# Attention inside an attention + MoE + MLP kernel: the reciprocal sums are transposed and multiplied onto the value products, instead of multiplying the exponentials

## The chip, the cores and the metric

One core of one Trainium2 chip runs the whole program. The metric is the device time of one execution, in microseconds (us). Times come from three timed runs of the kernel before and from one further execution that the hardware profiler recorded. Engines: TensorE (PE, with its weight loads as PEld), VectorE (DVE), ScalarE (ACT), GpSimd (POOL), and SyncE (SP), which issues most DMAs.

## The reference

```
B, H, S, D = 2, 8, 576, 64                      # attention
scores = q @ k.T / sqrt(D) + (cum[q] - cum[k])  # cum = cumsum(log(clip(f)))
scores = where(causal, -1e9, scores)
attn = exp(scores - max(scores))
attn = attn / (sum(attn) + 1e-9)
x = attn @ v                                    # -> [1152 tokens, 512]
p = domain_probs / sum(domain_probs)            # MoE: 4 experts, 512 -> 1024 -> 512
x = sum_e p[:, e] * (relu(x @ w1[e]) @ w2[e])
h = x @ w_in; g = h * sigmoid(1.702 * h)        # MLP: 512 -> 2048 -> 512
return g @ w_out
```

The step that the change touches is the division by the row sum: the kernel before divides the exponentials, the changed one divides `attn @ v`.

## The kernel before, in words

The tokens form four chunks `c`: 256 and 320 tokens of each of the two batches. Attention goes by pairs of heads, in three passes: chunk 0 (four pairs), chunk 1 (four pairs), then chunks 2 and 3 together (four pairs). A pair is cut into units. In chunk 0 a unit is one head with two tiles of 128 queries. In the other chunks a unit is one tile of 128 queries for both heads of the pair; the last tile of chunks 1 and 3 holds 64 queries of each head and is 576 keys wide (here "the 576 unit"; the units before it are the 384 and the 512 unit, after the width of their scores).

The generator `attention()` advances by one unit per step ("pull"). Step `i` emits, in this order: the value product `emit_pv` and the hand-over `emit_x2` of a pair whose last unit was `i-3`; the transposes `emit_tr` of unit `i-2`; exponential `emit_exp` and normalisation `emit_norm` of unit `i-1`; scores `emit_scores` and the maximum pass `emit_max` of unit `i`. So the exponentials of a unit are transposed two steps after its scores. Also in that step the keys, queries and decay rows of a pair three units ahead are prepared on GpSimd (`prep_parts`: tiles `khi`, `klo`; `prep_queries`: `qhi`, `qlo`; `prep_cum`: tiles `cb`, `cbs`, whose rows come by a broadcast DMA from `cumd` and get the causal triangle added), and the next pair's inputs are loaded on SP's queue.

For one unit the chain is: scores (PE, tile `s`), maximum with the decay added (DVE, `e`, `mx`), exponential with its sum (ACT, `e`, `sm`), sum + 1e-9 and its reciprocal (DVE, L454 and L455), multiplication of the exponentials by it (POOL, L457), transposes (PE, tile `t`, L475), copies to `ph` (ACT, in chunk 0 half of them DVE), and per pair the value product (PE, tile `x`, L505), rounding to `xh` (ACT), remainder `xl` (DVE, L514).

Between pulls the main loop emits expert products. Each is twelve matmuls in three groups of four (high parts, low weights, low activations). The weights come as `wst` by DMA and are split: the high part `whi` on ACT or POOL, the low part `wlo` on DVE (L165). `emit_first` is a block of 48 products that stands after the eleventh pull. After attention only expert and MLP products are left.

TensorE executes in the order of the program text. The other engines' orders are set by a scheduler at compile time; each engine then runs its list strictly in order, so an instruction that waits holds up all behind it.

Of the kernel before, what the change touches and what calls it, by code (L numbers as in the profile page):

```python
# [7 lines left out]
F32 = mybir.dt.float32  # L8
# [3 lines left out]
ALU = mybir.AluOpType  # L12
# [3 lines left out]
NT = B * S  # L16
DM = 512
SA = 256
SB = S - SA
CH = [(0, 0, SA), (0, SA, SB), (1, 0, SA), (1, SA, SB)]  # L20
NCH = len(CH)

WN = 384
WIDE = [NCH, NCH + 1, NCH + 2]
KW = S + 128
# [8 lines left out]
def attn_moe_mlp(ctx: ExitStack, tc: tile.TileContext, qk0, qk1, qk2, v0, vp, fg, dp, wa_moe, wb_moe, wa_mlp, wb_mlp, outT):  # L34
# [6 lines left out]
    nc = tc.nc  # L41

    def pool(name, bufs, space=None, scope=ctx):
        kw = {} if space is None else {"space": space}
        return scope.enter_context(tc.tile_pool(name=name, bufs=bufs, **kw))

    def f(ap):
        return ap.bitcast(F32)
# [4 lines left out]
    def round_act(out, in_):  # L53
        nc.scalar.activation(out=out, in_=in_, func=AF.Copy)  # L54

    const = pool("const", 1)
# [5 lines left out]
    tmp_p = pool("tmp", 2)  # L62
# [6 lines left out]
    xh, xl = ([t[:, :, t0:t0 + n] for t0, n in span] for t in (xh_t, xl_t))  # L69
# [11 lines left out]
    att_scope = ctx.enter_context(ExitStack())  # L81
    ac = pool("ac", 1, scope=att_scope)
    hi_p = pool("hi", 2, scope=att_scope)
    qhi_p = pool("qhi", 3, scope=att_scope)
    kq_p = pool("kq", 3, scope=att_scope)
    v_p = pool("v", 3, scope=att_scope)
    cb_p = pool("cb", 4, scope=att_scope)
    cbs_p = pool("cbs", 2, scope=att_scope)
    e_p = pool("e", 3, scope=att_scope)
# [159 lines left out]
        dpb[e] = t  # L249

    def load_probabilities():
        raw = const.tile([128, NT // 32], F32, name="dpraw")
        nc.sync.dma_start(out=raw, in_=dp)
        return raw

    def make_probabilities(raw):

        out = const.tile([128, 4, NT // 128], F32, name="dpn")
        s = const.tile([128, NT // 128], F32, name="dps")
        v = raw.rearrange("p (j e) -> p e j", e=4)  # L260
        nc.gpsimd.tensor_add(s, v[:, 0], v[:, 1])
        for e in (2, 3):
            nc.gpsimd.tensor_add(s, s, v[:, e])
        nc.gpsimd.tensor_scalar(out=s, in0=s, scalar1=1e-9, scalar2=1.0, op0=ALU.add, op1=ALU.mult)
        nc.vector.reciprocal(out=s, in_=s)
        nc.gpsimd.tensor_mul(out, v, s.unsqueeze(1).to_broadcast([128, 4, NT // 128]))
        nc.sync.dma_start(out=dpT.rearrange("e (p j) -> p e j", p=128), in_=out)
# [23 lines left out]
    def plain(c):  # L291


        return c == 0
# [24 lines left out]
    def load_heads(p, h0):  # L319

        cs, b, s0 = p
        st = pairs[p, h0] = {}
        src = (qk2 if b else qk1)[h0 // 2]
        st["kq"] = kq_p.tile([128, KW], F32, tag="kq", name="kq")
        nc.sync.dma_start(out=st["kq"], in_=src[:, :KW])
        for i, c in enumerate(cs):
            st["q", c] = kq_p.tile([128, QW], F32, tag="qr", name="qr")
            nc.sync.dma_start(out=st["q", c], in_=src[:, KW + i * QW:KW + i * QW + QW])
        st["vd"] = v_p.tile([128, 5, 2, D], F32, tag="vd", name="vd")
        nc.sync.dma_start(out=st["vd"], in_=vp[b * H // 2 + h0 // 2].rearrange("p (t g d) -> p t g d", t=5, g=2))  # L330

# [17 lines left out]
    def prep_cum(p, h0):  # L349

        cs, b, s0 = p
        st = pairs[p, h0]
        r = b * H + h0
        st["cb"] = []
        for g in range(2):
            cb = cb_p.tile([128, 896], F32, tag="cb", name="cb")
            nc.sync.dma_start(out=cb[:, :512], in_=cumd[r + g:r + g + 1, :512].to_broadcast([128, 512]))

            nb = (384 - s0) // 128
            nc.gpsimd.tensor_add(cb[:, 512 + s0:896].rearrange("p (t k) -> p t k", t=nb),  # L360
                                 cb[:, s0:384].rearrange("p (t k) -> p t k", t=nb),
                                 tri.unsqueeze(1).to_broadcast([128, nb, 128]))
            nc.gpsimd.tensor_add(cb[:, 384:512], cb[:, 384:512], tri)
            st["cb"].append(cb)
        st["cbs"] = cbs_p.tile([128, S], F32, tag="cbs", name="cbs")
        nc.sync.dma_start(out=st["cbs"], in_=cumd[r:r + 2, :].unsqueeze(1).to_broadcast([2, 64, S]))
        for g in range(2):
            z = slice(64 * g, 64 * g + 64)
            nc.gpsimd.tensor_add(st["cbs"][z, 512:], st["cbs"][z, 512:], tri[z, z])
# [81 lines left out]
    def emit_norm(c, u):  # L451
        e, sm, todo = sc[c, u]
        k = len(todo)
        nc.vector.tensor_scalar(out=sm[:, 1, :k], in0=sm[:, 0, :k], scalar1=1e-9, scalar2=None, op0=ALU.add)  # L454
        nc.vector.reciprocal(out=sm[:, 0, :k], in_=sm[:, 1, :k])  # L455
        for i, (q0, off, w, _) in enumerate(todo):
            nc.gpsimd.tensor_scalar(out=e[:, off:off + w], in0=e[:, off:off + w], scalar1=sm[:, 0, i:i + 1],  # L457
                                    scalar2=1.0, op0=ALU.mult, op1=ALU.mult)

    def emit_tr(c, u):  # L460

        hs, tiles = u
        s0 = CH[c][1]
        e, sm, todo = sc.pop((c, u))
        for h in hs:
            if (c, h) not in ph_of:
                ph_of[c, h] = pt_p.tile([128, 4, SB], F32, tag="ph", name="ph")
        for k, (q0, off, w, _) in enumerate(todo):
            o = q0 - s0
            nk = (w + 127) // 128  # L470

            for k0, k1 in [(0, min(nk, 4))] + [(4, 5)] * (nk > 4):
                pt = ps_t.tile([128, 512], F32, tag="t", name="t")
                for i in range(k0, k1):
                    nc.tensor.transpose(pt[:, 128 * (i - k0):128 * (i - k0) + 128], e[:, off + 128 * i:off + 128 * i + 128], ident)  # L475
                cols = pt[:, :128 * (k1 - k0)].rearrange("p (i q) -> p i q", q=128)
                for j, h in enumerate(hs if w == S else hs[k:k + 1] if len(hs) > 1 else hs):
                    r = 64 if w == S else 128
                    ph = ph_of[c, h]
                    ph = ph[:, 3:4, 0:64] if k0 else ph[:, 0:k1, o:o + r]  # L480
                    if plain(c) and k1 == 2:
                        nc.vector.tensor_copy(ph, cols[:, :, j * r:(j + 1) * r])
                    else:
                        round_act(ph, cols[:, :, j * r:(j + 1) * r])
# [22 lines left out]
    def emit_x2(c, h):  # L507
        n = CH[c][2]
        if h % 2 == 1:
            k = h // 2  # L510
            x = xf.pop((c, k))[:, :n]
            x_made[0] += 1
            round_act(xh[c][:, k, :], x)
            nc.vector.tensor_sub(xl[c][:, k, :], x, f(xh[c][:, k, :]))  # L514

    STAGES = dict(scores=0, max=0, exp=1, norm=1, tr=2, pv=3, x2=3)
    L_X2 = STAGES["x2"]
# [5 lines left out]
    def attention():  # L523


        seq = unit_seq
        first, last = {}, {}
        for i, (c, u) in enumerate(seq):
            for h in u[0]:
                first.setdefault((pass_of[c], h - h % 2), i)  # L530
                last[c, h] = i
        first = {k: i for k, i in first.items() if k[0][2] or k[0][1]}
        first_q = {}
        for i, (c, u) in enumerate(seq):
            if not plain(c):
                first_q.setdefault((pass_of[c], u[0][0], c), i)
        nxt = list(first)
        per_unit = dict(scores=emit_scores, max=emit_max, exp=emit_exp, norm=emit_norm, tr=emit_tr)
        by_last = dict(pv=emit_pv, x2=emit_x2)
        names = sorted(STAGES, key=lambda k: -STAGES[k])  # L540
        for i in range(len(seq) + L_X2 + 1):
            done = None
            new = [k for k in nxt if first[k] == i + LEAD]
            for k in new:
                prep_parts(*k)
            for k in [k for k, j in first_q.items() if j == i + LEAD]:
                prep_queries(*k)
            for k in new:
                prep_cum(*k)
            for k in names:  # L550
                j = i - STAGES[k]
                if k in per_unit:
                    if 0 <= j < len(seq):
                        per_unit[k](*seq[j])
                    continue
                fn, at = by_last[k], last
                for key in list(at):
                    if at[key] == j:
                        fn(*key)
                        if k == "x2" and key[1] == H - 1:  # L560
                            done = key[0]
            for k in new:
                n = nxt.index(k) + 1
                if n < len(nxt):
                    load_heads(*nxt[n])
            yield done
# [162 lines left out]
    for i, (kind, v_, b, c) in enumerate(seq):  # L729
# [6 lines left out]
        for g in range(4):  # L736
            ev = early[g] if i == 0 else (emit_l1 if kind == 1 else emit_l2)(v_, b, c, g)
            n = 0
# [82 lines left out]
```

## Time and profile before

| | |
|---|---|
| time, median of 3 runs | 764.94 us (764.49 to 766.62) |
| the profiled execution: time, span from first to last instruction | 763.8 us, 762.1 us |
| busy in the span: PE, PEld, DVE, ACT, POOL | 714.2, 684.2, 457.7, 270.5, 293.4 us |
| mean granted TensorE clock, share of full | 0.989 |

The span is what the trace covers; the profiled execution's own time is 1.7 us longer than it, and 1.1 us shorter than the median. Busy time of PE counts overlapping matmuls once. Every instruction of an engine has a start, a duration, and, where the engine sat idle before it, the instruction whose end released it.

### The profile page before, as it was taken

What the parts mean: (1) busy time and instruction counts of PE and PEld (TensorE: products, weight loads), DVE (VectorE), ACT (ScalarE), POOL (GpSimd) and SP (SyncE); (2) the same over time, 40 slices, a digit from 0 to 9 for tenths busy, and PEclk for the clock granted to TensorE, in tenths of its full rate; (3) what the DMA queues carried; (4) which work ended last, traced back from release to release, by engine and by line L of the source; (5) the groups of instructions that cost most, each with busy time, mean ns of one, the idle gap of its engine ahead of it and who ended that gap; (6) DMA issues with size and microseconds to landing.
All of it is one profiled execution on the core that took longest, in us unless ns stands there. A gap on an engine that the chain in (4) does not pass through costs nothing.

```text
span 762.1 us, 11987 instructions
## 1 busy us (share of the span) xinstructions
PE 714.2 (94%) x4488; PEld 684.2 (90%) x4488; DVE 457.7 (60%) x1023; ACT 270.5 (35%) x629; POOL 293.4 (38%) x377
## 2 busy tenths in 40 slices
PE   4597778988999999999989999999999999999998
PEld 2375667977899999999989999999999999999998
DVE  4475366655674899999989934433893234324422
ACT  4355443455653223332122122212354443323420
POOL 6785666487342202232224423233352322222220
PEclk9998899999999999999999999999999999999999
DMA  9774354422133555545434311000100000000012
GB/s 300 216 194 149 125 145 140 128 99 67 56 111 89 187 164 180 183 139 164 116 108 139 110 56 56 1 0 1 56 1 1 1 1 1 0 1 1 1 42 83
DMA packets 31225, 68.81 MB, mean 90 GB/s; under 512 B 3224, under 2 KB 4768, under 8 KB 31168
## 3 DMA queue, kind: packets, MB, share of 16 engines
q1 hardware_dynamic: 31120, 68.01, 28.7%
q8 instruction: 35, 0.57, 0.3%
q14 instruction: 22, 0.18, 0.1%
q10 hardware_dynamic: 48, 0.05, 0.0%
HBM read 65.62 MB, written 2.41 MB: 89 GB/s over the span
## 4 chain that ended last, share of the span: by engine, by line
PE 56%; DVE 17%; DMA 15%; POOL 6%; issue 4%; ACT 1%; POOLq 0%; DVEq 0%; ACTq 0%; SPq 0%
PE m L625 27%; PE m L581 25%; DMA cbs<-cumd 4%; DMA mst<-in_wa_mlp_dram 4%; DMA mst<-in_wb_mlp_dram 3%; DVE wlo L165 3%; PE s L408 2%; DVE cvd L228 2%; DVE cvt L214 2%; DMA kq<-in_qk_dram 2%; PE t L475 2%; DVE wf L222 1%; POOL e L457 1%; DVE hl L608 1%; DVE tmp L639 1%
## 5 line engine op out<-in xcount | busy, mean ns | idle before, releaser
L641 POOL TENSOR_TENSOR acc<-acc,tmp 128x384 f32<-128x384 f32 (+3 forms) x112 | 113.7, 1027 | 250.2 <-DVE tmp L639 250.1
L625 PE MATMUL m<-hh,whi 128*128 128x384 f32 (+2 forms) x640 | 127.1, 320 | 0.8 <-DVE tmp L639 0.8
L625 PE MATMUL m<-hh,wlo 128*128 128x384 f32 (+2 forms) x640 | 127.0, 320 | 0.8 <-DVE wlo L165 0.8
L581 PE MATMUL m<-xh,whi 128*128 128x384 f32 (+2 forms) x624 | 125.0, 322 | 1.9 <-DVE hl L608 1.9
L625 PE MATMUL m<-hl,whi 128*128 128x384 f32 (+2 forms) x640 | 126.6, 319 | 0.0
L581 PE MATMUL m<-xh,wlo 128*128 128x384 f32 (+2 forms) x624 | 124.4, 321 | 0.0
L581 PE MATMUL m<-xl,whi 128*128 128x384 f32 (+2 forms) x624 | 124.4, 321 | 0.0
L165 DVE TENSOR_TENSOR wlo<-wst,whi 128x512 fp32r<-128x512 f32 x112 | 91.8, 821 | 34.1 <-ACT whi L54 19.6
L54 ACT ACTIVATE whi<-wst 128x512 fp32r<-128x512 f32 x103 | 64.6, 630 | 121.6 <-PE m L581 66.9
L625 PEld LDWEIGHTS m<-hh,whi 128*128 128x128 f32 x640 | 106.2, 189 | 1.3 <-DVE tmp L639 1.1
L625 PEld LDWEIGHTS m<-hh,wlo 128*128 128x128 f32 x640 | 105.9, 189 | 1.4 <-DVE wlo L165 1.4
L581 PEld LDWEIGHTS m<-xh,whi 128*128 128x128 f32 x624 | 103.9, 189 | 3.0 <-DVE hl L608 2.5
L625 PEld LDWEIGHTS m<-hl,whi 128*128 128x128 f32 x640 | 105.7, 189 | 0.0
L581 PEld LDWEIGHTS m<-xh,wlo 128*128 128x128 f32 x624 | 103.9, 189 | 0.0
L581 PEld LDWEIGHTS m<-xl,whi 128*128 128x128 f32 x624 | 103.9, 189 | 0.0
L616 POOL TENSOR_TENSOR hl<-tmp,hh 128x384 fp32r<-128x384 f32 x48 | 49.1, 1026 | 133.3 <-ACT hh L54 133.3
L607 ACT ACTIVATE hh<-m 128x384 fp32r<-128x384 f32 (+2 forms) x112 | 49.0, 437 | 124.9 <-PE m L581 124.0
L608 DVE SCALAR_TENSOR_TENSOR hl<-m,hh 128x384 fp32r<-128x384 f32 (+2 forms) x112 | 54.9, 492 | 36.5 <-ACT hh L607 36.5
L475 PE MATMUL t<-identr,e 128*128 128x128 f32 x200 | 36.7, 307 | 28.9 <-POOL e L457 28.6
L639 DVE TENSOR_TENSOR tmp<-m,dpb 128x384 f32<-128x384 f32 (+2 forms) x80 | 40.8, 511 | 32.7 <-PE m L625 30.6
L475 PEld LDWEIGHTS t<-identr,e 128*128 128x128 f32 x200 | 24.0, 151 | 39.8 <-POOL e L457 38.1
L448 ACT ACTIVATE e<-e,mx 128x128 f32<-128x128 f32 (+4 forms) x72 | 42.0, 584 | 49.3 <-DVE mx L434 43.8
(93 smaller groups left out, 763.5 us busy)
## 6 DMA issues: line engine op xcount, KB each, us to landing
wst<-in_wa_moe_dram SPq DMA_DIRECT2D x28, 512.0 KB, 3.7
wst<-in_wb_moe_dram SPq DMA_DIRECT2D x28, 512.0 KB, 3.9
mst<-in_wa_mlp_dram SPq DMA_DIRECT2D x16, 512.0 KB, 3.6
mst<-in_wb_mlp_dram SPq DMA_DIRECT2D x16, 512.0 KB, 3.5
cb<-cumd SPq DMA_DIRECT2D x16, 256.0 KB, 3.5
qr<-in_qk_dram SPq DMA_DIRECT2D x12, 256.0 KB, 4.5
kq<-in_qk_dram SPq DMA_DIRECT2D x8, 352.0 KB, 5.6
vd<-in_vp_dram SPq DMA_DIRECT2D x8, 320.0 KB
```

The costliest lines, as they stand in the source:

```text
L54: nc.scalar.activation(out=out, in_=in_, func=AF.Copy)
L165: sub = nc.vector.tensor_sub(lf, raw, f(hf))
L214: nc.vector.tensor_scalar(out=t, in0=hi, scalar1=0x7FFFFFFF, scalar2=None, op0=ALU.bitwise_and)
L448: nc.scalar.activation(out=e[:, off:off + w], in_=e[:, off:off + w], func=AF.Exp, scale=-1.0, bias=mx, accum_out=sm[:, 0, k:k + 1])
L475: nc.tensor.transpose(pt[:, 128 * (i - k0):128 * (i - k0) + 128], e[:, off + 128 * i:off + 128 * i + 128], ident)
L581: nc.tensor.matmul(p[:, :n], lhsT=w[:, k, :], rhs=x[c][:, k, :], start=(j == 0 and k == 0), stop=(j == 2 and k == 3))
L607: nc.scalar.activation(out=hh[:, g, :n], in_=p[:, :n], func=AF.Relu)
L608: nc.vector.scalar_tensor_tensor(out=hl[:, g, :n], in0=p[:, :n], scalar=0.0, in1=f(hh[:, g, :n]), op0=ALU.max, op1=ALU.subtract)
L616: nc.gpsimd.tensor_sub(hl[:, g, :n], t[:, :n], f(hh[:, g, :n]))
L625: nc.tensor.matmul(p[:, :n], lhsT=w[:, k, :], rhs=x[:, k, :n], start=(j == 0 and k == 0), stop=(j == 2 and k == 3))
L639: nc.vector.tensor_mul(t[:, :n], p[:, :n], d)
L641: nc.gpsimd.tensor_add(a, a, t[:, z])
```

## The change

The exponentials are no longer multiplied. Instead the reciprocal of each row's sum is written 64 times side by side (`rec`, 128 queries x 2 heads x 64). At the last transposes of a pair, `emit_rec` transposes `rec` into the same PSUM tile, which gives the reciprocals in the layout of the value product (head dimension in the partitions, queries along the row), and ACT copies them to `rt`. `emit_x2` multiplies the value product by `rt` on DVE into `xt`, rounds that, and takes the remainder on DVE for chunk 0 and on POOL for the others. To make room, `kq` and `vd` have two buffers in place of three, the values are loaded (`load_values`) at the first unit of their pair, and the expert probabilities use a `tmp` tile.

```diff
-    v_p = pool("v", 3, scope=att_scope)
+    xt_p = pool("xt", 2, scope=att_scope)
+    rec_p = pool("rec", 2, scope=att_scope)
+    v_p = pool("v", 2, scope=att_scope)
...
     def load_probabilities():
-        raw = const.tile([128, NT // 32], F32, name="dpraw")
-        nc.sync.dma_start(out=raw, in_=dp)
-        return raw
+        t = tmp_p.tile([128, WN], F32, tag="tmp", name="dpraw")
+        nc.sync.dma_start(out=t[:, :NT // 32], in_=dp)
+        return t
...
     def load_heads(p, h0):
-        st["kq"] = kq_p.tile([128, KW], F32, tag="kq", name="kq")
+        st["kq"] = kq_p.tile([128, KW], F32, tag="kq", name="kq", bufs=2)
...
+    def load_values(p, h0):
+        b = p[1]
+        st = pairs[p, h0]
         st["vd"] = v_p.tile([128, 5, 2, D], F32, tag="vd", name="vd")
         nc.sync.dma_start(out=st["vd"], in_=vp[b * H // 2 + h0 // 2].rearrange("p (t g d) -> p t g d", t=5, g=2))
...
     def emit_norm(c, u):
         e, sm, todo = sc[c, u]
         k = len(todo)
+        h = u[0][0]
+        if (c, h // 2) not in rec:
+            rec[c, h // 2] = rec_p.tile([128, 3, 2, 64], F32, tag="rec", name="rec")
+        r = rec[c, h // 2]
+        r = r[:, :2, h % 2, :] if plain(c) else r[:, (todo[0][0] - CH[c][1]) // 128]
         nc.vector.tensor_scalar(out=sm[:, 1, :k], in0=sm[:, 0, :k], scalar1=1e-9, scalar2=None, op0=ALU.add)
-        nc.vector.reciprocal(out=sm[:, 0, :k], in_=sm[:, 1, :k])
-        for i, (q0, off, w, _) in enumerate(todo):
-            nc.gpsimd.tensor_scalar(out=e[:, off:off + w], in0=e[:, off:off + w], scalar1=sm[:, 0, i:i + 1],
-                                    scalar2=1.0, op0=ALU.mult, op1=ALU.mult)
+        nc.vector.reciprocal(out=r, in_=sm[:, 1, :k].unsqueeze(2).to_broadcast([128, 2, 64]) if k == 2 else
+                             sm[:, 1, 0:1].unsqueeze(2).to_broadcast([128, 2, 64]))
+
+    rec, rcp = {}, {}
+
+    def emit_rec(c, h, pt, o):
+
+        r = rec.pop((c, h // 2))
+        n = CH[c][2]
+        for j in range(0, n, 128):
+            nc.tensor.transpose(pt[:, o + j:o + j + 128], r[:, j // 128].rearrange("p g d -> p (g d)"), ident)
+        t = rcp[c, h // 2] = xt_p.tile([128, SB], F32, tag="rt", name="rt", bufs=1)
+        round_act(t[:, :n], pt[:, o:o + n])
+        if n > 256:
+            round_act(t[64:, 256:n], pt[64:, o + n:o + n + 64])
 
     def emit_tr(c, u):
...
+                if k + 1 == len(todo) and hs[-1] % 2 and k1 == nk and q0 + 128 >= s0 + CH[c][2]:
+                    emit_rec(c, hs[0], pt, 128 * (k1 - k0))
...
     def emit_x2(c, h):
-            x = xf.pop((c, k))[:, :n]
+            p, r = xf.pop((c, k)), rcp.pop((c, k))
             x_made[0] += 1
+            x = xt_p.tile([128, SB], F32, tag="xt", name="xt")[:, :n]
+            nc.vector.tensor_mul(x, p[:, :n], r[:, :n])
             round_act(xh[c][:, k, :], x)
-            nc.vector.tensor_sub(xl[c][:, k, :], x, f(xh[c][:, k, :]))
+            (nc.vector if plain(c) else nc.gpsimd).tensor_sub(xl[c][:, k, :], x, f(xh[c][:, k, :]))
...
+            for k in nxt:
+                if first[k] == i:
+                    load_values(*k)
```

The scheduler's lists change with it, at three places that matter below.

GpSimd (POOL), around the preparation of the fourth pair of chunk 1: its `cbs` rows come by DMA, `klo` is its keys' low part, and `e<-e,sm` are multiplications of exponentials of the third pair (576 of the second pair's last unit first). First the rows of before, then those of the change.

```order
L51 TENSOR_SCALAR khi<-kq 128x704
L457 TENSOR_SCALAR e<-e,sm 128x576
L369 TENSOR_TENSOR cbs<-cbs,tri 64x64 x2
L338 TENSOR_TENSOR klo<-kq,khi 128x704
L425 MEMSET e 128x64
L51 TENSOR_SCALAR qhi<-qr 128x256 x2
L347 TENSOR_TENSOR qlo<-qr,qhi 128x256 x2
L457 TENSOR_SCALAR e<-e,sm 128x384 x2
```

```order
L51 TENSOR_SCALAR khi<-kq 128x704
L542 TENSOR_TENSOR xl<-xt,xh 128x320
L346 TENSOR_TENSOR klo<-kq,khi 128x704
L377 TENSOR_TENSOR cbs<-cbs,tri 64x64 x2
L51 TENSOR_SCALAR whi<-wst 128x512
L433 MEMSET e 128x64
L51 TENSOR_SCALAR qhi<-qr 128x256 x2
L355 TENSOR_TENSOR qlo<-qr,qhi 128x256 x2
```

The multiplications are gone from the list, the remainder `xl` of a pair has come in, and `klo` now stands ahead of the `cbs` rows.

VectorE (DVE), at the maximum pass of the 384 unit of the second pair of chunk 1 (the four `e,mx<-s,cb` rows), with low parts of weights and of the first expert block's activations (`hl`). First before, then the change.

```order
L608 SCALAR_TENSOR_TENSOR hl<-m,hh 128x256
L434 ISA e,mx<-s,cb 128x256
L434 ISA mx 128x1
L608 SCALAR_TENSOR_TENSOR hl<-m,hh 128x256
L434 ISA e,mx<-s,cb,mx 128x128
L434 ISA mx 128x1
L434 ISA e,mx<-s,cb 128x256
L434 ISA mx 128x1
L608 SCALAR_TENSOR_TENSOR hl<-m,hh 128x256
L165 TENSOR_TENSOR wlo<-wst,whi 128x512
L434 ISA e,mx<-s,cb,mx 128x128
```

```order
L167 TENSOR_TENSOR wlo<-wst,whi 128x512 x3
L639 SCALAR_TENSOR_TENSOR hl<-m,hh 128x256
L442 ISA e,mx<-s,cb 128x256
L442 ISA mx 128x1
L639 SCALAR_TENSOR_TENSOR hl<-m,hh 128x256
L442 ISA e,mx<-s,cb,mx 128x128
L442 ISA mx 128x1
L442 ISA e,mx<-s,cb 128x256
L442 ISA mx 128x1
L639 SCALAR_TENSOR_TENSOR hl<-m,hh 128x256
L442 ISA e,mx<-s,cb,mx 128x128
```

The low part that waits for a weight tile split on GpSimd stood behind three of the four maximum rows; now it is the last of the three `wlo` ahead of all four.

VectorE again, in chunk 0, near the value product of heads 4 and 5: `ph<-t` is the copy of transposed exponentials that the value product reads. First before, then the change.

```order
L455 RECIPROCAL sm<-sm 128x2
L165 TENSOR_TENSOR wlo<-wst,whi 128x512
L482 COPY ph<-t 128x2x128
L434 ISA e,mx<-s,ones 128x128
L434 ISA mx 128x1
L434 ISA e,mx<-s,ones 128x256
```

```order
L167 TENSOR_TENSOR wlo<-wst,whi 128x512
L468 RECIPROCAL rec<-sm 128x2x64
L508 COPY ph<-t 128x2x128
L467 TENSOR_SCALAR sm<-sm 128x2
L468 RECIPROCAL rec<-sm 128x2x64
L540 TENSOR_TENSOR xt<-x,rt 128x256
L508 COPY ph<-t 128x2x128
```

The reciprocal has 128 columns in place of 2, and the copy that the value product needs stands directly behind it.

## Rows read from the trace of the kernel before

**Rows 1.** Busy time by engine in four stretches, then granted clock, DMA share, GB/s.

```profile
0.00:45.00 45.00, 24.97 (x87) 15.25 (x87) 23.26 (x79) 17.62 (x53) 32.91 (x65) 1.00 0.77 241
45.00:130.00 85.00, 68.05 (x474) 59.24 (x475) 46.46 (x151) 43.03 (x116) 56.45 (x86) 0.90 0.50 148
130.00:225.00 95.00, 90.65 (x665) 81.91 (x664) 62.19 (x191) 54.13 (x146) 52.31 (x80) 1.00 0.30 94
225.00:762.00 537.00, 530.56 (x3267) 527.82 (x3265) 325.76 (x606) 155.73 (x314) 151.71 (x147) 1.00 0.22 68
```

**Rows 2.** TensorE's waits over the span: us in total, times, longest.

```profile
PE t L475 <- POOL e L457: 28.6, 17, 5.2
PE s L408 <- DMA kd<-fr: 9.1, 1, 9.1
PE s L408 <- DVE mx L434: 2.8, 2, 2.3
```

**Rows 3.** The same wait within 0:45, 45:130 and 130:225, one row each.

```profile
PE t L475 <- POOL e L457: 10.5, 5, 5.2
PE t L475 <- POOL e L457: 13.9, 5, 4.5
PE t L475 <- POOL e L457: 4.3, 7, 1.1
```

**Rows 4.** Timeline of chunk 1's third pair: start, us, engine, line, [idle before, releaser].

```profile
70.32 0.50 SPq L366 DMA_DIRECT2D cbs<-cumd  x1
75.03 0.61 ACT L448 ACTIVATE e<-e,mx 128x384 f32<-128x384 f32 x1
78.44 1.23 POOL L369 TENSOR_TENSOR cbs<-cbs,tri 64x64 f32<-64x64 f32 x2 [5.17 <-DMA cbs<-cumd]
83.60 1.16 POOL L457 TENSOR_SCALAR e<-e,sm 128x384 f32<-128x384 f32 x2
84.24 1.54 PE L475 MATMUL t<-identr,e 128*128 128x128 f32 x6 [4.53 <-POOL e L457]
```

**Rows 5.** Windows after that wait, columns as in Rows 1.

```profile
84.00:87.00 3.00, 2.76 (x12) 2.69 (x13) 0.00 (x0) 0.98 (x2) 0.77 (x3) 0.50 0.86 215
87.00:90.00 3.00, 3.00 (x16) 3.00 (x16) 1.31 (x6) 1.04 (x3) 3.00 (x5) 0.51 0.85 322
90.00:93.00 3.00, 3.00 (x24) 3.00 (x24) 2.25 (x8) 1.96 (x5) 3.00 (x4) 1.00 0.17 58
```

**Rows 6.** Groups by shape up to 225 us: count, busy us, mean ns, idle before.

```profile
L455 DVE RECIPROCAL sm<-sm 128x2 f32<-128x2 f32 x32 | 5.2, 164 | 0.9
L265 DVE RECIPROCAL dps<-dps 128x9 f32<-128x9 f32 x1 | 0.2, 215 | 0.1
L434 DVE CUSTOM_DVE_ANT_0 e<-s,ones 128x128 f32<-128x128 f32 x8 | 2.3, 287 | 4.7 <-PE s L408 4.5
L636 DVE TENSOR_TENSOR acc<-m,dpb 128x320 f32<-128x320 f32 x4 | 2.0, 492 | 1.4 <-PE m L625 1.4
L641 POOL TENSOR_TENSOR acc<-acc,tmp 128x320 f32<-128x320 f32 x2 | 2.3, 1127 | 4.8 <-DVE tmp L639 4.8
L54 ACT ACTIVATE ph<-t 128x256 f32<-128x256 f32 x22 | 7.3, 378 | 1.0 <-PE t L475 0.8
```

**Rows 7.** Eight transposes in a row, TensorE's weight loads.

```profile
54.52 0.90 PEld L475 LDWEIGHTS t<-identr,e 128*128 128x128 f32 x8
```

**Rows 8.** Timeline of chunk 1's second pair, from its decay rows' DMA to its scores.

```profile
50.52 0.51 SPq L366 DMA_DIRECT2D cbs<-cumd  x1
59.78 0.70 POOL L369 TENSOR_TENSOR cbs<-cbs,tri 64x64 f32<-64x64 f32 x2 [1.35 <-DMA cbs<-cumd]
60.58 0.62 POOL L51 TENSOR_SCALAR whi<-wst 128x512 fp32r<-128x512 f32 x1
61.23 0.69 DVE L165 TENSOR_TENSOR wlo<-wst,whi 128x512 fp32r<-128x512 f32 x1 [1.46 <-POOL whi L51]
62.34 0.76 PE L408 MATMUL s<-khi,qhi 128*128 128x512 f32 x1 [2.34 <-DVE mx L434]
```

More of the change, by code (lines that the diff above doesn't have):

```diff
@@ L251, in load_probabilities, with make_probabilities @@
     def load_probabilities():
-        raw = const.tile([128, NT // 32], F32, name="dpraw")
-        nc.sync.dma_start(out=raw, in_=dp)
-        return raw
[L256 to L260, printed above, removed]
+        t = tmp_p.tile([128, WN], F32, tag="tmp", name="dpraw")
+        nc.sync.dma_start(out=t[:, :NT // 32], in_=dp)
+        return t
+    def make_probabilities(t):
+        w = NT // 32
+        out = t[:, w:2 * w].rearrange("p (e j) -> p e j", e=4)
+        s = t[:, 2 * w:2 * w + NT // 128]
+        v = t[:, :w].rearrange("p (j e) -> p e j", e=4)
         nc.gpsimd.tensor_add(s, v[:, 0], v[:, 1])
```

## The prediction, made before the changed kernel ran

> **What bounds the kernel now.** I read the busy time by stage first [rows 1]. From 225 us on TensorE is busy 530.6 of 537 us, so nothing that the change does to another engine can help there; only TensorE's own work and its idle time ahead of 225 us count. In 0 to 45 us it is busy 25.0 of 45, in 45 to 130 us 68.1 of 85, in 130 to 225 us 90.7 of 95. Then the waits of TensorE [rows 2]: 9.1 us at the start for the first inputs, which the change leaves alone, and 28.6 us in 17 waits of transposes for the multiplication on GpSimd, the instruction that the change removes. By stage these are 10.5, 13.9 and 4.3 us [rows 3].
>
> Why GpSimd is late shows in the timeline of one pair [rows 4]. The exponentials of the 384 unit start on ScalarE at 75.03 and take 0.61 us, so they are ready at about 75.7. Their multiplication starts only at 83.60, since GpSimd's list has the decay rows `cbs` ahead of it, whose DMA was issued at 70.32 and landed at 78.44 (8.1 us), and then the preparation of the next pair. TensorE idles 4.53 us before the transposes at 84.24. [...]
>
> **The change, part by part.** The sum is made for the profiled execution (763.8 us, 1.1 us below the median).
>
> *Removed: the waits for the multiplication, 28.6 us.* Transposes then wait for the exponentials, which in the example are ready 8 us earlier.
>
> *Clock given back, 4 us.* Before, 45 to 130 us holds 68.1 us of work at a mean of 0.90. If the engine is at half speed for a share s of 85 us, the mean is 1 - s/2, so s is 0.2, or 17 us, and 8.5 us would be regained if it never fell. One of the stalls stays (below), so I take half, 4 us; bounds 0 and 8.5.
>
> *Added on TensorE: 40 transposes of reciprocals.* Two per pair in chunks 0 and 2, three in chunks 1 and 3, four pairs each: 8 + 12 + 8 + 12. Eight in a row take 0.90 us [rows 7], 0.11 each: 0.9, 1.3 and 2.2 us in the three stages, 4.4 us in all. They stand in the order of the program, so nothing hides them.
>
> *The reciprocal, on VectorE.* 40 instructions go from 2 columns to 128. No row has that form. From 2 to 9 columns it grows from 164 to 215 ns [rows 6], 7.3 ns a column; carried on to 128 this is 164 + 126 x 7.3 = 1.08 us. The other bound is a pass that takes one column after the other, 287 ns for 128 columns in the maximum pass. I take 1.08, since it is the same instruction's slope, though from one instance. Extra VectorE time: 40 x 0.92 = 37 us, or 5 us at the low bound. [...]
>
> *Also on VectorE:* 16 products with a PSUM operand (0.49 each, as L636 [rows 6]) come, 7.8 us; 12 remainders of about that length leave for GpSimd. There they take about 1.13 us each (as L641), 13.5 us in all, in the room left by the multiplications. Their readers are expert products many units later; without that room they could delay the next `khi` by 1 us per pair. ScalarE gets 16 copies (0.38 us by the 256-column row) and 8 short ones, some 8 us. It is busy 54.1 of 95 us in the third stage [rows 1], so these hide, if their turn in the list does not come before the transposes are done; then the exponentials behind them are late by as much as the reciprocal is.
>
> *First stage, new waits of 9 us.* I walked VectorE's list through chunk 0 with the durations above. Two kinds of waits appear. The value product needs the VectorE copy that now stands behind a 1.08 us reciprocal and a low part (third pair of order lists): for heads 0 and 1, 2 and 3, 4 and 5 TensorE waits 1.7, 0.3 and 2.9 us. And the transposes of `rec` need the last reciprocal of the pair: for heads 2 and 3 it stands behind two low parts and a remainder, 3.1 us. With some short ones I get 8.8, taken as 9. Bounds: 2.5 with reciprocals of 0.29, 12 if each of the eight reciprocals cost 0.92 once more where I saw cover. Gain of the stage: 10.5 - 0.9 - 9 = 0.6 us.
>
> *Second stage, new waits of 5 us.* The second pair of chunk 1 gets worse. Its chain: `cbs` DMA 50.52 to 59.78, then on GpSimd the rows and a weight split until 61.2, then VectorE's low part until 61.9 [rows 8]. Before, one maximum row of the 384 unit stood behind this, and TensorE waited 2.34 us for the score tiles. Now all four stand behind it with three `hl` among them, so I get the tiles free at about 63.1, with TensorE ready at 57.2: 5.9 us, 3.6 more than before. 1.5 us go to waits for the third reciprocal of a pair. In the third and fourth pairs I found nothing late: the `klo` that the next scores need stands ahead of the `cbs` rows now, and the reciprocal is done about 1 us ahead of the transposes. Gain: 13.9 + 4 - 1.3 - 5 = 11.6 us. Bounds of the new waits: 3.6 and 13.
>
> *Third stage, new waits of 2 us.* Removed 4.3, added 2.2. VectorE goes from 62.2 busy us of 95 to about 62 + 18 x 0.92 = 79, 83%. TensorE's expert products need their PSUM tiles emptied by it, so some waits must come: 2 us, bounds 0 and 18.4 (20 reciprocals all in line). Gain 0.1 us.
>
> *Loads, nothing.* `vd` (320 KB) is now issued at its pair's first unit and read three units later, 11 us or more; a DMA here lands within 8.1 to 9.3 us of its issue in the slowest rows [rows 4, 8]. If that cover were gone each late load would cost 1 to 2 us. It is also moved behind a wait for an earlier value product on SP's queue, and the `cbs` DMA stands behind it; that product is over before the maximum that `cbs` itself waits for. `kq` with two buffers waits for a preparation that is already done. The probabilities' tile is in use only before any expert output needs it.
>
> Sum: 0.6 + 11.6 + 0.1 = 12.3 us, 763.8 - 12.3 = 751.5 us. On the median's scale 764.9 - 12.3 = **752.6 us**.
>
> **The rivals.**
> *A cheap reciprocal.* If 128 columns take about 0.29 us, the first stage's new waits fall from 9 to 2.5, the third's from 2 to 0 and the 1.5 us of the second go: 12.3 + 10 = 22 us gained, 743. For it speaks that elementwise passes take 287 ns; against it, the slope in [rows 6].
> *The waits only move to the decay rows' DMA.* The 8 us broadcast [rows 4] is still there, and VectorE reaches it through weight low parts split on GpSimd behind `cbs`, as in the second pair [rows 8]. If the third and fourth pairs wait so too, the second stage gives some 1.5 us and nothing of the clock: 0.6 + 1.5 + 0.1 = 2.2, 762.7, no change that counts. Against it: in the third pair's list only one such split is left, and its maximum pass comes 4 us later.
> *VectorE becomes the limit in the third stage; slower.* At 83% busy and in strict order, its reciprocals could hold the emptying of PSUM: 20 x 0.92 = 18.4 us on the path in place of my 2, a gain of 12.3 - 16.4 = -4.1, 769 us. It decides from 14.3 us of such waits, 15 of the 20. For it speaks that remainders and products of expert tiles share the list; against it, that TensorE had almost no wait for them in the trace before [rows 2].
>
> **How the numbers follow.** Chances: forecast 0.66, cheap reciprocal 0.09, moved waits 0.11, VectorE-bound 0.14. A difference of 0.3% (2.3 us) is about what these runs can tell. The forecast is faster nearly always, the cheap reciprocal always, the moved waits half and half with no change: faster 0.76, same 0.10, slower 0.14. The range goes from 743.5, which leaves out most of the cheap reciprocal, to 766.5, which leaves out most of the VectorE-bound case. The likeliest case's own range is 746 to 760, from the clock's bounds and the first stage's.
>
> **What would show it.** Right: no wait of transposes for GpSimd; reciprocals of 128 columns near 1.08 us; TensorE waiting for VectorE copies and `rec` in the first 45 us, and about 6 us for a maximum pass near 57 us; the block of 48 products ending within 1 us of 54.5; the first scores of chunk 2, at 108.4 us before, 10 to 12 us earlier; the expert stage unchanged in length. Wrong: new waits of expert products for VectorE above a few us between 120 and 215 us, a first stage that grows, or a clock that stays low in the third and fourth pairs.

## The result and the profile after

The changed kernel takes 754.17 us (median of 4 runs, 752.44 to 755.41) against 765.76 us (4 runs, 764.49 to 766.62): ratio 0.9848, 95% interval 0.9818 to 0.9879, so 11.6 us faster by the ratio, where 752.6 was predicted. Its profiled execution took 755.33 us, its span is 753.5 us, 8.6 us shorter than the span before. One of the four runs of experiment 2 below (803.2 us) fell in a slower state and is left out of every figure. The total is close to the forecast; the places where the time was won and lost are not.

TensorE's waits over the span of the changed kernel (us in total, times, longest), which answer to [rows 2, 3]:

```profile
PE s L416 <- DVE mx L442: 14.7, 9, 7.6
PE s L416 <- DMA kd<-fr: 10.2, 1, 10.2
PE m L612 <- DVE hl L639: 3.8, 1, 3.8
PE t L478 <- DVE rec L468: 3.3, 1, 3.3
PE x L531 <- DVE ph L508: 1.7, 1, 1.7
```

No transpose waits for GpSimd any more. Scores now wait 14.7 us for maximum passes, 12.4 of it between 45 and 130 us, and expert products 3.8 us for `hl`. The windows, which answer to [rows 1]:

```profile
0.00:45.00 45.00, 27.38 (x109) 19.36 (x109) 32.20 (x87) 19.42 (x59) 26.60 (x52) 0.89 0.80 244
45.00:130.00 85.00, 68.71 (x490) 60.01 (x489) 55.00 (x149) 44.36 (x123) 42.64 (x64) 0.90 0.49 147
130.00:225.00 95.00, 95.00 (x713) 88.86 (x713) 73.22 (x194) 57.56 (x159) 39.66 (x58) 1.00 0.34 104
```

In the third window TensorE never idles. In the second it is as busy as before (68.7 us against 68.1), and its clock is 0.90 again. In the first the granted clock, 1.00 before, is 0.89.

Where did the second stage's gain go? Three pieces of the timeline (start, us, engine, line, [idle before, releaser]), each from the decay rows' DMA to the TensorE instruction that waits:

```profile
47.92 0.51 SPq L374 DMA_DIRECT2D cbs<-cumd  x1
59.40 0.70 POOL L377 TENSOR_TENSOR cbs<-cbs,tri 64x64 f32<-64x64 f32 x2 [2.96 <-DMA cbs<-cumd]
60.19 0.62 POOL L51 TENSOR_SCALAR whi<-wst 128x512 fp32r<-128x512 f32 x1
60.84 0.69 DVE L167 TENSOR_TENSOR wlo<-wst,whi 128x512 fp32r<-128x512 f32 x1 [4.71 <-POOL whi L51]
62.96 0.77 PE L416 MATMUL s<-khi,qhi 128*128 128x512 f32 x1 [7.61 <-DVE mx L442]
...
85.90 0.51 SPq L374 DMA_DIRECT2D cbs<-cumd  x1
95.65 0.70 POOL L377 TENSOR_TENSOR cbs<-cbs,tri 64x64 f32<-64x64 f32 x2 [5.50 <-DMA cbs<-cumd]
96.44 0.62 POOL L51 TENSOR_SCALAR whi<-wst 128x512 fp32r<-128x512 f32 x1
97.10 0.69 DVE L167 TENSOR_TENSOR wlo<-wst,whi 128x512 fp32r<-128x512 f32 x1 [8.08 <-POOL whi L51]
98.45 1.29 PE L416 MATMUL s<-khi 128*128 128x288 f32 x2 [3.46 <-DVE mx L442]
...
112.40 0.71 POOL L377 TENSOR_TENSOR cbs<-cbs,tri 64x64 f32<-64x64 f32 x2 [2.59 <-DMA cbs<-cumd]
115.34 0.62 POOL L51 TENSOR_SCALAR whi<-wst 128x512 fp32r<-128x512 f32 x1
115.99 0.69 DVE L167 TENSOR_TENSOR wlo<-wst,whi 128x512 fp32r<-128x512 f32 x1 [4.22 <-POOL whi L51]
121.13 0.74 PE L612 MATMUL m<-xh,whi 128*128 128x256 f32 x4 [3.80 <-DVE hl L639]
```

The chain is the same three times: GpSimd waits for the rows, a weight split stands behind them in its list, VectorE's low part waits for that split, and the maximum passes or `hl` that TensorE needs stand behind the low part. TensorE loses 7.6, 3.5 and 3.8 us. The scores are those of the 512 unit of chunk 1's second pair and of the 576 unit of its fourth; the products at 121 us lie inside the first pair of chunks 2 and 3. The rows fetched belong to the pair after, since preparation runs three units ahead.

The groups by shape up to 225 us (count | busy us, mean ns | idle before), which answer to [rows 6]:

```profile
L468 DVE RECIPROCAL rec<-sm 128x128 f32<-128x128 f32 x40 | 38.1, 952 | 1.1
L540 DVE TENSOR_TENSOR xt<-x,rt 128x320 f32<-128x320 f32 x7 | 3.3, 465 | 2.0 <-PE x L531 2.0
L542 POOL TENSOR_TENSOR xl<-xt,xh 128x320 fp32r<-128x320 f32 x7 | 6.1, 875 | 12.4 <-ACT xh L54 12.4
```

### The profile page after: what moved, and what is told of

Its sections match the earlier page's. It is cut to its first block, busy times and chain, and to the rows that moved or that the text cites. A ratio compares the mean times of both kernels' runs of the same rounds, so it can differ in the third digit from the quotient of the medians.

```text
span 753.5 us, 11964 instructions
## 1 busy us (share of the span) xinstructions
PE 714.7 (95%) x4528; PEld 689.3 (91%) x4528; DVE 482.7 (64%) x1027; ACT 275.3 (37%) x653; POOL 256.5 (34%) x317
## 4 chain that ended last, share of the span: by engine, by line
PE 73%; DVE 12%; DMA 10%; issue 2%; POOL 1%; ACT 1%; SPq 0%; DVEq 0%; POOLq 0%; ACTq 0%
PE m L656 32%; PE m L612 31%; PE s L416 5%; DMA cbs<-cumd 4%; PE x L531 3%; DMA mst<-in_wb_mlp_dram 3%; DMA mst<-in_wa_mlp_dram 3%; PE t L499 2%; DVE wlo L167 2%; DVE cvd L230 2%; DVE cvt L216 1%; DVE e L442 1%; DVE hl L639 1%; DVE wf L232 1%; DMA kd<-fr 1%
## 5 line engine op out<-in xcount | busy, mean ns | idle before, releaser
L167 DVE TENSOR_TENSOR wlo<-wst,whi 128x512 fp32r<-128x512 f32 x112 | 89.7, 803 | 31.8 <-POOL whi L51 17.2
L54 ACT ACTIVATE whi<-wst 128x512 fp32r<-128x512 f32 x103 | 64.6, 630 | 123.6 <-PE m L612 68.1
L645 DVE TENSOR_TENSOR tmp<-m,sg 128x384 f32<-128x384 f32 x48 | 26.6, 554 | 54.2 <-ACT sg L644 54.2
L167 DVE TENSOR_TENSOR wlo<-wf,whi 128x512 fp32r<-128x512 f32 x32 | 24.9, 779 | 28.0 <-ACT whi L54 26.9
```

What stands on the lines that cost most here:

```text
L167: sub = nc.vector.tensor_sub(lf, raw, f(hf))
L645: nc.vector.tensor_mul(t[:, :n], p[:, :n], s[:, :n])
```

## The experiments

Theory A: the missing gain went to that chain, whose root is the decay rows' DMA. Theory B: the added VectorE work, 40 reciprocals of 0.95 us, gave it back. In the table, the waits are TensorE's for other engines in 0 to 45, 45 to 130 and 130 to 225 us (without the first inputs' DMA), and the clock is that of 45 to 130 us. The last column is the time from the first to the fourth pair's value products of chunk 2, the same stretch of the program in each. Each ratio is to the kernel before timed beside that run (medians 765.8 to 767.4 us), so small differences are read from the ratios.

| kernel | us (range) | ratio to before, 95% | waits, us | clock | chunks 2, 3 |
|---|---|---|---|---|---|
| before | 765.8 | 1 | 10.5, 17.1, 4.3 | 0.90 | 63.92 |
| changed | 754.17 (752.4 to 755.4) | 0.9848 (0.9818 to 0.9879) | 7.3, 16.2, 0 | 0.90 | 58.62 |
| 1 splits on ScalarE | 740.93 (738.8 to 741.2) | 0.9672 (0.9638 to 0.9705) | 5.5, 3.9, 0 | 0.96 | 58.62 |
| 2 the same in before | 759.0 (758.2 to 760.5) | 0.9893 (0.9871 to 0.9915) | 9.9, 15.2, 3.7 | 0.92 | 63.39 |
| 3 rows by two DMAs | 738.33 (737.1 to 739.6) | 0.9641 (0.9614 to 0.9669) | 7.2, 6.4, 0 | 0.96 | 58.62 |
| 4 the same in before | 745.13 (743.0 to 748.0) | 0.9731 (0.9695 to 0.9766) | 7.2, 5.7, 1.7 | 0.96 | 60.35 |
| 5 short reciprocal | 745.0 (742.5 to 746.6) | 0.9728 (0.9687 to 0.9769) | 5.3, 11.4, 0 | 0.94 | 58.62 |
| 6 reciprocal twice | 763.92 (761.6 to 766.7) | 0.9978 (0.996 to 0.9996) | 7.1, 17.7, 2.8 | 0.86 | 63.54 |
| 7 both 1 and 5 | 734.64 (733.1 to 736.9) | 0.9593 (0.9547 to 0.9639) | 5.1, 3.5, 0 | 0.98 | 58.62 |
| 8 and copy on ScalarE | 734.03 (733.5 to 737.0) | 0.9562 (0.9545 to 0.958) | 3.7, 6.9, 0 | 0.96 | 58.62 |
| 9 and clearing on VectorE | 735.25 (734.0 to 737.0) | 0.9601 (0.9576 to 0.9626) | 3.1, 2.5, 0 | 0.98 | 58.62 |
| 10 before, no multiplication | 745.74 (743.8 to 746.9) | 0.9715 (0.9694 to 0.9735) | 4.7, 12.6, 0 | 0.94 | 57.03 |
| 11 transposes twice | 754.89 (751.2 to 757.4) | 0.9833 (0.9799 to 0.9866) | 6.7, 14.1, 0 | 0.90 | 60.32 |
| 12 before, loads alone | 762.33 (760.3 to 763.9) | 0.9954 (0.9939 to 0.997) | 8.7, 16.9, 3.2 | 0.90 | 62.77 |

**1. Weight splits on ScalarE.**

```diff
-            (round_pool if v_ <= 2 and g == 3 else round_act)(hf, raw)
+            round_act(hf, raw)
```

> The changed kernel, with the three splits of weight tiles that still stand on GpSimd behind the decay rows given to ScalarE. Theory A (the gain that is missing in the second stage went to the decay rows' DMA: GpSimd waits for it, the weight split stands behind it, VectorE's low part behind that, and the maximum passes or activations behind that): the three TensorE waits of 7.6, 3.5 and 3.8 us for VectorE near 57, 97 and 119 us shrink to under 1.5 us each, no VectorE idle time is ended by a GpSimd weight split after the first 45 us, and the time falls from 754 to 741 to 747 us, with some low-clock time gone too. Theory B (the added VectorE work, 40 reciprocals of 0.95 us, gave the gain back): waits of the same sum, only elsewhere; 752 to 756 us.

13 us faster than the changed kernel. TensorE's waits between 45 and 130 us:

```profile
PE s L416 <- DVE mx L442: 2.4, 3, 2.1
PE m L612 <- ACT hh L638: 1.5, 1, 1.5
```

They fall by 12.3 us, to 3.9, and the clock of that stage rises to 0.96. The decay rows still land as late: GpSimd still waits for them, in this trace up to 7.2 us at a time, but nothing that TensorE needs soon stands behind it. One wait of 2.1 us is longer than the 1.5 that A allowed, and 740.9 us is just below its range; otherwise A holds, and B does not explain this.

**2. The same edit in the kernel before.**

> The kernel before, with the same three kinds of weight splits given to ScalarE. Theory A (the decay rows' wait was covered before by the wait for GpSimd's multiplication, and only came to the path when that left): the multiplications still wait for the decay rows on GpSimd, so only the 2.3 us wait of the second pair and the split's own 0.6 us can go: 760 to 765 us. Rival: the placing of the splits is worth its 13 us in any kernel: 750 to 755 us.

8 us by the ratio, more than A's 5 at most and less than the rival's 10; the median of 759.0 us lies between the two ranges. The transposes still wait 27.1 us for GpSimd's multiplication (9.7, 13.7 and 3.7 by stage). So the splits did cost something before, and 5 us more once the multiplications were gone.

**3. The decay rows by two DMAs** of one head, 64 partitions each, in the changed kernel.

```diff
-        nc.sync.dma_start(out=st["cbs"], in_=cumd[r:r + 2, :].unsqueeze(1).to_broadcast([2, 64, S]))
+        for g in range(2):
+            z = slice(64 * g, 64 * g + 64)
+            nc.sync.dma_start(out=st["cbs"][z, :], in_=cumd[r + g:r + g + 1, :].to_broadcast([64, S]))
```

> The changed kernel with the decay rows fetched by two DMAs of one head each in place of one of both heads; nothing else differs. Theory A: if they land earlier than the 8 to 10 us of now, the three waits of TensorE for VectorE near 57, 97 and 119 us shrink by about as much as the landing, 742 to 750 us for 3 to 4 us each; if they land as late, 752 to 757 us and the same three waits. Theory B (VectorE's load) expects 752 to 757 us in either case.

The largest gain of any single edit to the changed kernel, 16 us beyond it. The profile's list of DMAs (count, KB each, median us from issue to landing) and the waits between 45 and 130 us:

```profile
cbs<-cumd SPq DMA_DIRECT2D x16, 144.0 KB, 4.6
...
PE s L418 <- DVE mx L444: 6.2, 4, 4.3
PE m L658 <- DVE hl L641: 0.2, 1, 0.2
```

Each of the two DMAs lands in 4.6 us (median), where the single one above took 9.75 from issue to use (85.90 to 95.65). The splits stay on GpSimd, and the waits of the fourth pair and at 121 us are gone. The one near 57 us falls from 7.6 to 4.3 us, by the 3 to 4 us that A wanted. What is left there is no wait for the rows: GpSimd adds the triangle at 52.59 us without having been idle, behind its own preparation. No work left VectorE, so B cannot explain it. The time beats A's 742 to 750.

**4. The same two DMAs in the kernel before.**

> The kernel before, with the decay rows fetched by two DMAs of one head each and nothing else changed; it shows what is left for removing the multiplications once the rows land in some 4.6 us. If the multiplications were late because of the rows' DMA, their waits in the second stage fall from 13.9 us to 3 to 6 us and in the third from 4.3 to under 3, while the 10.5 us of the first stage stay: 748 to 757 us, so that most of the second stage's gain of the change was to be had without it. If they were late because GpSimd itself has too much to do (a pair of multiplications takes 1.2 to 2 us there): waits over 10 us in the second stage, 759 to 765 us.

Faster than expected: 745.1 us, better than the change itself. The first stage's waits, expected to stay at 10.5 us, fell too. TensorE's waits for the multiplication, by stage:

```profile
PE t L477 <- POOL e L459: 6.7, 4, 3.7
...
PE t L477 <- POOL e L459: 4.4, 5, 1.7
...
PE t L477 <- POOL e L459: 1.7, 3, 1.0
```

12.8 us in place of 28.6. So more than half of the waits that the change removed were waits for this DMA, passed on by GpSimd's list. With the rows quick, the change is still worth about 7 us (745.1 to 738.3, ratios 0.9731 and 0.9641).

**5. A short reciprocal**, of 1 or 2 columns, copied to 128 on VectorE.

```diff
-        nc.vector.reciprocal(out=r, in_=sm[:, 1, :k].unsqueeze(2).to_broadcast([128, 2, 64]) if k == 2 else
-                             sm[:, 1, 0:1].unsqueeze(2).to_broadcast([128, 2, 64]))
+        nc.vector.reciprocal(out=sm[:, 0, :k], in_=sm[:, 1, :k])
+        nc.vector.tensor_copy(r, sm[:, 0, :k].unsqueeze(2).to_broadcast([128, 2, 64]) if k == 2 else
+                              sm[:, 0, 0:1].unsqueeze(2).to_broadcast([128, 2, 64]))
```

> The changed kernel, with the reciprocal taken of 1 or 2 columns and then copied to 128 columns on VectorE. The pair should cost about 0.16 + 0.2 to 0.3 us in place of 0.95, some 20 us less of VectorE work. Theory A (decay rows): the waits of the first stage for rec and for the copy behind it (3.3 and 1.7 us) mostly go, the three waits behind the decay rows stay: 748 to 752 us. Theory B (VectorE's load): the waits for VectorE fall in all stages, 738 to 745 us.

9 us faster than the changed kernel, in B's range by a hair and better than A's. Its VectorE groups:

```profile
L469 DVE COPY rec<-sm 128x128 f32<-128x128 f32 x40 | 14.0, 349 | 0.8
L468 DVE RECIPROCAL sm<-sm 128x2 f32<-128x2 f32 x32 | 5.2, 163 | 0.8
```

0.16 + 0.35 us replace 0.95, 17.6 us less in all. But the waits for `mx` and `hl` between 45 and 130 us only fall from 16.2 to 11.1 us: the chain stays. VectorE's load is a second cause, smaller than the first.

**6. Every reciprocal twice**, by the same line once more.

```diff
+        nc.vector.reciprocal(out=r, in_=sm[:, 1, :k].unsqueeze(2).to_broadcast([128, 2, 64]) if k == 2 else
+                             sm[:, 1, 0:1].unsqueeze(2).to_broadcast([128, 2, 64]))
```

> The changed kernel with every reciprocal of 128 columns done twice, 38 us more of VectorE work (about 8 us in the first 45 us, 12 between 45 and 130, 18 after). Theory A: it shows mainly in the first stage, where the last reciprocal of a pair is waited for: 3 to 8 us, 757 to 762 us, nothing after 130 us. Theory B: VectorE is as good as on the path, over 15 us, above 768 us.

9.8 us slower than the changed kernel, between the two. A is wrong on the place: the third stage grows too, where VectorE is now busy 82.5 of 95 us. TensorE's waits there:

```profile
PE t L480 <- DVE rec L470: 1.6, 2, 1.3
PE s L416 <- DVE mx L442: 1.2, 3, 0.5
```

The last column of the table grows from 58.6 to 63.5 us. B is wrong on the size: 37 us more of VectorE work cost 10.

**7 to 9. Edits 1 and 5 together; then the copy on ScalarE; then also the clearing of the last 64 columns of `e` (L433) on VectorE.**

```diff
-        nc.vector.tensor_copy(r, sm[:, 0, :k].unsqueeze(2).to_broadcast([128, 2, 64]) if k == 2 else
+        round_act(r, sm[:, 0, :k].unsqueeze(2).to_broadcast([128, 2, 64]) if k == 2 else
...
-                        nc.gpsimd.memset(e[:, S:640], 0.0)
+                        nc.vector.memset(e[:, S:640], 0.0)
```

> The changed kernel with both edits: weight splits on ScalarE, and the reciprocal of 1 or 2 columns with a copy. Theory A: the sum of the two, 737 to 744 us, TensorE's waits for VectorE under 4 us after the first 45 us. Theory B: no better than the short reciprocal alone, to within 2 us.

> The changed kernel with the splits on ScalarE and the short reciprocal, its 128 columns now written by a copy on ScalarE in place of VectorE: 15 us less of VectorE work than the kernel with both edits (734.6 us). If VectorE's list still holds TensorE in the first stage (4.2 us of waits for the reciprocals there): 730 to 733 us. If ScalarE's list, which has the exponentials, takes its place: 735 to 741 us, with waits for exponentials or for ScalarE's copies in the first 45 us.

> The changed kernel with splits on ScalarE, short reciprocals copied on ScalarE (734.0 us so far), and the clearing of the last 64 columns of the 576 unit, for which transposes waited 3.9 us since it stands on GpSimd behind the decay rows, given to VectorE. Theory A (anything short on GpSimd behind the decay rows' DMA that TensorE or VectorE needs puts that DMA on the path): that wait goes, 728 to 732 us. Rival (those transposes are as late for another reason): 733 to 736 us.

Both edits give 734.6 us, 19.5 less than the change (13.2 and 9.2 alone): they mostly add, against B, and the time is below A's range. With the copy on ScalarE nothing clear of the noise is gained, and the time lies between the two that were expected: the waits for reciprocals fall from 4.2 us to 1.0, but a new one comes, for the clearing that stands on GpSimd behind the rows:

```profile
PE t L500 <- POOL e L433: 3.9, 1, 3.9
```

Moving the clearing takes that row away, as A said, yet the time (735.25) lies in the rival's range and not below that of experiment 8. Why is open; the profiled span of experiment 9 (732.3 us against 735.2) is shorter, its timed runs are not. The three cannot be told apart. They are the fastest measured, 31 us under before. Their combination with the two DMAs was not tried.

**10. The kernel before without the multiplication.**

```diff
-        for i, (q0, off, w, _) in enumerate(todo):
-            nc.gpsimd.tensor_scalar(out=e[:, off:off + w], in0=e[:, off:off + w], scalar1=sm[:, 0, i:i + 1],
-                                    scalar2=1.0, op0=ALU.mult, op1=ALU.mult)
```

> The kernel before without the multiplications of the exponentials on GpSimd; the division is left out altogether, sums and reciprocals of 2 columns stay. It shows what the removed wait alone is worth. Theory A: 28.6 us of waits go and some 10 to 15 us come back behind the decay rows, since the weight splits still stand on GpSimd: 742 to 750 us. Rival (what came back in the changed kernel came from its new instructions on VectorE and TensorE): 765 less 28.6 less 4 to 8 of the clock, 728 to 733 us.

As A expected. TensorE's waits between 45 and 130 us:

```profile
PE s L408 <- DVE mx L434: 9.4, 4, 6.4
PE m L578 <- DVE hl L605: 3.2, 1, 3.2
```

The waits of transposes for GpSimd go, and these 12.6 us for `mx` and `hl` come without any new VectorE work: taking the multiplication away is enough to bring the chain out. The changed kernel, which divides elsewhere, is 8 us slower than this one (10 by the ratios): that is the price of all that the change adds, its loads included.

**11. Each transpose of reciprocals twice.**

```diff
+            nc.tensor.transpose(pt[:, o + j:o + j + 128], r[:, j // 128].rearrange("p g d -> p (g d)"), ident)
```

> The changed kernel with each of the 40 transposes of reciprocals done twice. By the row that priced them, 0.11 us each, 4.4 us more if nothing hides them: 757.5 to 760 us. If waits of TensorE that stand right behind take them up: 754 to 757 us. If at the lower clock and with their weight loads they cost twice as much: 761 to 764 us.

No change of the time that can be measured; 754.9 us is in the second of the three ranges. Where TensorE never idles the price shows: the last column is 60.32 us in place of 58.62, 1.70 us for 15 instructions, 0.11 each. What hid the rest in the first two stages is open; TensorE's waits there are 2.7 us shorter.

**12. The kernel before with the changed loads alone.**

```diff
-    v_p = pool("v", 3, scope=att_scope)
+    v_p = pool("v", 2, scope=att_scope)
...
-        st["kq"] = kq_p.tile([128, KW], F32, tag="kq", name="kq")
+        st["kq"] = kq_p.tile([128, KW], F32, tag="kq", name="kq", bufs=2)
...
+            for k in nxt:
+                if first[k] == i:
+                    load_values(*k)
```

> The kernel before with the changed loads alone: two buffers for keys and for values, and the values loaded at the first unit of their pair. The prediction says nothing: 0.997 to 1.003 of before, 764 to 769 us. Rival (the values' 320 KB are now issued a few microseconds ahead of the decay rows and make those land later, and the multiplications behind them wait longer): 769 to 774 us, with the decay rows landing 1 to 2 us later than in the kernel before.

Both were wrong: 3.5 us faster by the ratio. The waits for the multiplication are 24.3 us (8.2, 12.9 and 3.2) in place of 28.6. Which of the loads does it was not separated.

## Why the prediction was right, and where it was not

The bound and the removed wait were right. That the total came close was luck: the second stage gave nothing of the 11.6 us forecast for it, and three gains that were put at 0.6 us or less made up for most of that.

**The bound and the wait.** Right: most of the gain, 6.9 of 8.6 us on the span, lies ahead of chunk 2's last value products (212.78 us before), and the 28.6 us of [rows 2] are gone.

**The step that failed: the second stage.** "In the third and fourth pairs I found nothing late" held for the third pair only. The fourth lost 3.5 us, and the first pair of the next pass, which was not walked, 3.8. The second pair's wait was found by its chain, 5.9 us, and measured 7.6. TensorE's waits for VectorE in this stage went from 3.2 us to 16.2: 13.0 new, in place of 5, at the edge of the bounds (3.6 and 13). With 13.0 and with no clock regained the prediction's own sum gives 13.9 + 0 - 1.3 - 13.0 = -0.4 us in place of 11.6. The rival "the waits only move to the decay rows' DMA" is what happened there, in the second stage, and had a chance of 0.11. Its time for the whole kernel, 762.7, did not come, since the other stages gave more than it granted. Experiments 1 and 3 show it by cutting the chain at two different links. What misled stands in the prediction: the 8 us DMA was seen in [rows 4], and the split behind it in [rows 8], but the DMA's length was taken as given and the list was walked for pairs, not for each place where a split stands behind the rows.

**Clock, 4 us.** The 4 us was the author's estimate, half of the 8.5 us that the mean of 0.90 [rows 1] gives if the low clock is half of full speed; no run shows it. Over the stage nothing came back: 0.90 in both. From 80 to 90 us, where it had been 0.50 to 0.51 after 84 [rows 5], it is now 1.00; but it is 0.66 from 55 to 70 us, around the 7.6 us wait, and 0.81 from 121 to 130, behind the 3.8 us wait. The step rested on one remaining stall, and three remained (7.6, 3.5 and 3.8 us). A loss in the first stage (1.00 to 0.89) was not in the sum at all.

**First stage, 0.6 us.** The last value product of chunk 0 starts at 44.17 in place of 46.55, 2.4 us earlier, though the first inputs landed 1.1 us later. Waits of 7.3 us in place of 9: `rec` for heads 2 and 3 waited 3.3 (3.1 predicted), heads 4 and 5 waited 1.7 for their copy (2.9 predicted), the rest was score tiles. The block of 48 products ends at 52.5 us, outside the 1 us around 54.5 that was to show the forecast right. The loads, put at nothing, may be part of this: alone (experiment 12) they bring that value product to 45.61, 0.9 us earlier.

**Third stage, 0.1 us.** The largest part of the gain. The first and the fourth pair's value products of chunk 2, before and then in the changed kernel:

```profile
148.86 0.87 PE L505 MATMUL x<-ph,vd 128*64 128x256 f32 x8
212.78 0.87 PE L505 MATMUL x<-ph,vd 128*64 128x256 f32 x8
...
147.25 0.87 PE L531 MATMUL x<-ph,vd 128*64 128x256 f32 x8
205.87 0.87 PE L531 MATMUL x<-ph,vd 128*64 128x256 f32 x8
```

They lie 63.9 us apart before and 58.6 after, so 5.3 us are won. The new waits were 0, not 2: VectorE was busy 73 of 95 us, not 79. And without multiplications and transposes alike (experiment 10) the stretch takes 57.0: 6.9 us less than before, of which 4.3 had shown as waits. The other 2.6 us are busy time of TensorE that became shorter. Its 75 transposes of exponentials in the stretch, before and in the changed kernel (count | busy us, mean ns | idle before):

```profile
L475 PE MATMUL t<-identr,e 128*128 128x128 f32 x75 | 12.5, 286 | 4.4 <-POOL e L457 4.3
L499 PE MATMUL t<-identr,e 128*128 128x128 f32 x75 | 11.0, 277 | 0.0
```

That transposes split up by the arrival of one head after the other take longer is argued, not shown.

**Sum.** On the span of the profiled executions: first stage +2.4 (0.6 predicted), from there to the first value products of chunk 2 -0.8 (11.6 predicted for the second stage), from there to the fourth +5.3 (0.1 predicted), the rest +1.7 (nothing predicted): 8.6 in place of 12.3. The second stage fell 12.4 us short and the others gave 8.7 more, so errors of opposite sign brought the total close. The first scores of chunk 2, which were to come 10 to 12 us earlier, came 5.1 earlier (103.32 for 108.42), and most of that went in the 3.8 us wait at 121 us, a sign that the prediction had named as one of being wrong. In the rest TensorE's waits fall from 3.1 us to 1.4; the loads alone do that too (1.3 in experiment 12), so "nothing" for the loads was short by about that much.

**Prices.** The transposes were right, 0.11 us (58.62 less 57.03 for 15, experiment 10). The reciprocal took 0.952 us, 1.08 predicted: (952 - 164) / 126 is 6.3 ns a column, not the 7.3 of the slope in [rows 6]. The remainders on GpSimd took 0.875 us for 320 columns, 1.13 predicted. The cheap reciprocal as a rival was priced at 10 us; experiment 5 gave 9.2.

**VectorE-bound third stage.** It did not come, but was not far: in experiment 6 VectorE is busy 9 us more of those 95, and the stretch takes 4.9 us longer.

## What to carry to other kernels

Before an instruction that waits is taken away, ask what it waits for: here more than half of the waits for GpSimd's multiplications came from a DMA awaited ahead of them in the same list, and removing them handed the lateness to the next reader. Walk the list of the waiting engine for everything that stands behind the slow transfer, in every round of the loop. And look first at why the transfer is slow: its repair alone gave more (20.6 us by the ratio of experiment 4) than the change (11.6 us).

## What the runs showed of the hardware

The decay rows' DMA of 288 KB took 8 to 11.5 us from issue to use where GpSimd sat waiting for it ([rows 4, 8], and 11.5 us at 47.92 and 9.75 at 85.90 above); the 256 KB of `cb` land in 3.2 (the median in the changed kernel's list of DMAs). While it is the last in flight, the window's DMA share (the column before GB/s) is 0.12 to 0.13, at 47 to 53 GB/s. The last two rows are from experiment 3, whose two DMAs were issued at 153.57 us:

```profile
94.00:95.00 1.00, 1.00 (x12) 0.69 (x8) 0.00 (x0) 0.00 (x0) 0.00 (x0) 1.00 0.13 53
95.00:96.00 1.00, 0.00 (x0) 0.00 (x0) 0.00 (x0) 0.00 (x0) 0.31 (x1) 1.00 0.12 47
...
155.00:156.00 1.00, 1.00 (x9) 1.00 (x9) 1.00 (x5) 0.55 (x2) 1.00 (x2) 1.00 0.70 219
156.00:157.00 1.00, 1.00 (x9) 0.99 (x8) 0.20 (x3) 0.81 (x4) 1.00 (x3) 1.00 0.17 46
```

At 50 GB/s, between the 47 and 53 of the first two rows, 295 KB (288 of 1,024 bytes) take an estimated 5.9 us to move. DMAs of 64 partitions (144 KB each) landed in 4.6 us in experiment 3 and 3.7 in experiment 4 (medians). From 155 to 156 us experiment 3 had a share of 0.70 and 219 GB/s, more than five times the share of the single DMA. What keeps the single DMA at so small a share is shown by no run.
